# Score products of the first two head pairs from zero-padded parts written in place, second pair rotated on GpSimd

## The chip, the cores and the metric

One core of a Trainium2 chip runs the kernel. The metric is the device time of one execution in microseconds; several executions are timed and their median is taken. One more execution is recorded by the hardware profiler, and all rows of this document come from such a recording. The engines are TensorE (PE, with its weight loads shown apart as PEld), VectorE (DVE), ScalarE (ACT), GpSimd (POOL) and the DMA queue of SyncE (SP). Each engine works through its own instructions in the order in which the program lists them.

## The reference

Attention with rotary embedding on 32 heads (4 batches of 8), 576 positions of 64 channels, followed by a one-of-eight expert layer and a dense layer:

```
q_rot, k_rot = (rotate(q), rotate(k))
scores = scale * np.matmul(q_rot, k_rot.transpose(0, 1, 3, 2))
scores = scores - np.max(scores, axis=-1, keepdims=True)
attn = np.exp(scores)
attn = attn / (np.sum(attn, axis=-1, keepdims=True) + 1e-09)
return np.matmul(attn, v).astype(np.float32)
...
x = _moe_ref(x=x, **moe_kwargs)
return _moe2_ref(x=x, **moe2_kwargs)
```

where `rotate` is `[x1*cos - x2*sin, x1*sin + x2*cos]` on the two halves of the channels. The expert layer sends each of 2304 rows through one expert (512 to 1024 to 512, ReLU); the dense layer is 512 to 2048 to 512 with squared ReLU.

## The kernel before

**Stages.** The program does attention first (about the first 290 us), then the routing and the experts, then the dense layer. The change is in the attention stage alone, in its first microseconds.

**Pairs.** Attention works on 16 pairs of heads, P = 0 to 15. The two heads of a pair stand on partitions 0 to 63 and 64 to 127. The tile `qk` (two buffers) holds keys and queries of a pair, once as they are and once with the halves of the channels swapped, so `rotate` (L189) is three elementwise passes: two products with the table `TB` (L392 in the helper `times`) and a sum (L388 in `plus`). The 128 rotary positions left over from 576 = 512 + 64 of both heads share one block of 128 columns.

**Two parts.** The products on TensorE are taken with numbers of type fp32r, and the precision comes from splitting each rotated value: `high` (L195) writes the rounded value to `XH` on ACT, `low` (L202) writes the remainder to `XL`. A score is H·H + L·H + H·L (query part times key part). A head has only 64 channels, half of the array's rows, so `stack_up` (L212) copies parts by DMA into stacked tiles: `kZ` holds the head's H keys twice, above each other, and `qZ` the H queries above the L queries. One product of `qZ` with `kZ` then gives H·H + L·H, and a second one, of `QH` (H queries of one head, zeros on the other head's partitions) with `XL`, gives H·L. That is 8 DMAs per pair.

**Scores.** `scores(P, s)` (L228) makes one block of 128 queries by 576 keys in two halves of 288 columns, into one of two PSUM buffers `ps`. There are nine blocks per pair: s = 0 to 3 for the first head, 4 to 7 for the second, and 8 for the leftover queries of both (two stacked products and one more a half). Then `smax` (L251, DVE) takes the row maximum and `sexp` (L258, ACT) the exponential, after which the PSUM buffer is free. The exponentials are transposed on TensorE (`turn`, L276), copied to SBUF by DVE or ACT (L292, L294), multiplied with V (`values`, L303), and projected together with the gate weights (`project`, L314).

**Order.** Nothing reorders the program at run time. `prepare` (L140) issues the first pair's work, then every later step is put on a list with a due time (`at`, `OFF`, `pair` = 15.954 a pair) and the list is issued in order of due time. The due time decides only the place in each engine's row. For pair 2 and later, `rotate` runs on POOL, `high` on ACT, `low` on POOL, and `stack_up` on SP. Pairs 0 and 1 are done in `prepare`, with `rotate` on DVE. After the first `high`, 16 products on a scratch tile `warm` (L162) keep TensorE occupied until the first stacked tiles arrive.

Of the kernel before, what the change touches and what calls it, by code (L numbers as in the profile page):

```python
# [10 lines left out]
F32 = mybir.dt.float32  # L11
F32R = mybir.dt.float32r
# [100 lines left out]
def attention(tc, rope, ident, qk, v, w_gate, xd, on_batch, later):  # L113
# [14 lines left out]
    T = {}  # L128
# [11 lines left out]
    def prepare():  # L140
        nc.scalar.dma_start(out=TB[:, :, 0], in_=rope)
        load(0)
        load(1)
        for t in Xs:
            nc.gpsimd.memset(t[:, 576:640], 0.0)
        for t in SS:
            nc.gpsimd.memset(t[:, :, 1:2], 1e-9)
        for two in QH:
            for j in range(2):
                nc.gpsimd.memset(two[j][64 - 64 * j:128 - 64 * j].bitcast(F32), 0.0)  # L150
        nc.gpsimd.memset(R, 0.0)
        for r in range(2):
            d = slice(64 * r, 64 * r + 64)
            nc.gpsimd.tensor_copy(R[d, :, r, 0:64], ident[d, d].unsqueeze(1).broadcast_to([64, 4, 64]))
        for o, lo, hi in ((0, 64, 640), (576, 0, 64)):
            nc.scalar.activation(TB[:, :, 1, o:o + hi - lo], TB[:, :, 0, lo:hi], AF.Copy, scale=0.125)
        for n in range(2):
            rotate(0, n, nc.vector)
            high(0, n)
        w = ppt("warm")  # L160
        for i in range(16):
            nc.tensor.matmul(w, T["hi", 0][:, 0, 0:128], T["hi", 0][:, 0, 0:512], start=True, stop=True)  # L162
        for n in range(2):
            low(0, n, nc.vector)
            stack_up(0, n)
        load(2)
        rotate(1, None, nc.vector)
        high(1)
        low(1)
        load_v(0)  # L170
        for r in range(2):
            nc.sync.dma_start(out=R[64 * r:64 * r + 64, :, r, 64:72], in_=w_gate.rearrange("(g r d) e -> r d g e", r=2, d=64)[r])
        later()
        stack_up(1)

    def load(P):
        t = T["qk", P] = ldp.tile([128, 2, 2, 640], F32, name="qk", tag="qk", bufs=2)
# [7 lines left out]
    def load_v(P):  # L185
        V = T["V", P] = ldp.tile([128, 2, 5, 64], F32, name="V", tag="V", bufs=2)
        nc.sync.dma_start(out=V, in_=v[P].rearrange("p (h c d) -> p h c d", h=2, c=5))

    def rotate(P, n, eng, step=None):  # L189
        x, a = T["qk", P], slice(0, 2) if n is None else slice(n, n + 1)  # L190
        for i, (f, o, y) in enumerate(((times, 0, TB[:, 0, a]), (times, 1, TB[:, 1, a]), (plus, 0, x[:, 1, a]))):
            if step in (None, i):
                f(eng, x[:, o, a], x[:, o, a], y)

    def high(P, n=None):  # L195

        if ("hi", P) not in T:
            T["hi", P] = wp.tile([128, 2, 640], F32R, name="XH", tag="XH", bufs=2)
        a = slice(0, 2) if n is None else slice(n, n + 1)
        nc.scalar.activation(T["hi", P][:, a], T["qk", P][:, 0, a], AF.Copy)  # L200
# [27 lines left out]
    def scores(P, s):  # L228

        t = T["S", P, s] = ps.tile([128, 2, 512], F32, name="ps", tag="ps", bufs=2)  # L230
        if s < 8:
            j, c = divmod(s, 4)
            todo, qs, qh = [j], slice(c * 128, c * 128 + 128), QH[P % 2][j]
            qh = qh[:, qs]
        else:
            todo, qs, qh = [0, 1], slice(512, 640), T["hi", P][:, 1, 512:640]
        k0 = 0 if s in (4, 5, 6, 7) else 64
        for i, j in enumerate(todo):
            Q1, K1 = T["qZ", 2 * P + j], T["kZ", 2 * P + j]
            for u in range(2):  # L240
                nc.tensor.matmul(t[:, u, 0:288], Q1[:, qs], K1[:, k0 + 288 * u:k0 + 288 * u + 288], start=i == 0, stop=False)  # L241
        for u in range(2):
            nc.tensor.matmul(t[:, u, 0:288], qh, T["lo", P][:, 0, k0 + 288 * u:k0 + 288 * u + 288], start=False, stop=True)  # L243
# [103 lines left out]
            at(t, lambda: route(P, t))  # L347

    prepare()
    for P in range(NPAIR):  # L350
        def on(o, f, *args):
            at(OFF["pair"] * P + o, lambda: f(*args))

        if P > 2:
            on(OFF["load"], load, P)
        if P > 0:
            on(OFF["v"], load_v, P)
        if P > 1:
            for i in range(3):
                on(OFF["rope"] + 2.93 * i, rotate, P, None, nc.gpsimd, i)  # L360
            on(OFF["hi"], high, P)
            on(OFF["lo"], low, P)
            on(OFF["z"], stack_up, P)
        for s in range(9):
            on(OFF["S"][s], scores, P, s)
            on(OFF["max"][s], smax, P, s)
            on(OFF["exp"][s], sexp, P, s)
        for un, o, o2 in zip(UNITS, OFF["un"], OFF["out"]):
            on(o, turn, P, un)
            on(o2, turned, P, un)  # L370
        for u in range(2):
            on(OFF["av"][u], values, P, u)
            on(OFF["x"][u], gathered, P, u)
        on(OFF["pj"], project, P)
        on(OFF["fin"], finish, P)
        if P % 4 == 3:
            on(OFF["fin"] + .02, route, P)
# [659 lines left out]
```

## Time and profile before

| | us |
|---|---|
| median of 3 timed executions | 1027.9 (1024.9 to 1030.28) |
| the profiled execution | 1029.81 |
| its span in the trace | 1028.0 |
| PE busy | 981.3 (95%) |
| DVE busy | 547.3 (53%) |
| ACT busy | 420.6 (41%) |
| POOL busy | 310.4 (30%) |

The profiled execution took 1.9 us more than the median, and 1.8 us of it lie outside the span. Busy times are of the whole span; matmul ends are modelled, so a busy PE need not be at its peak. The granted clock (PEclk) is the share of TensorE's full 2.4 GHz: 1.00 is that level, 0.50 is 1.2 GHz. Where the trace has no event of the clock yet, at the start, the column says 1.00 whatever the level was.

### The profile page before, as it was taken

The numbers are of one execution on the slowest core, as the hardware profiler recorded it, in microseconds if no ns is written. First come the engines' busy times: TensorE is split into PE (matmuls) and PEld (weight loads), VectorE is DVE, ScalarE is ACT, GpSimd is POOL, SyncE is SP. The second block draws the span as 40 slices with busy tenths as digits, with TensorE's granted clock in tenths as the row PEclk, the third lists the DMA queues.
The fourth block names the chain that finished last, engine by engine and source line by source line (L and its number), as shares of the span: only waits on it lengthen the run. The fifth ranks groups of instructions, "written<-read, shape, count | busy, mean of one in ns | idle before, by whom it ended". The sixth has DMA issues, their size and how long they took to land. (4 is left out here: it accounts for less than half of the span.)

```text
span 1028.0 us, 15645 instructions
## 1 busy us (share of the span) xinstructions
PE 981.3 (95%) x5624; PEld 838.2 (82%) x5624; DVE 547.3 (53%) x909; ACT 420.6 (41%) x825; POOL 310.4 (30%) x211
## 2 busy tenths in 40 slices
PE   4999999999997999999999988899999999999998
PEld 3788888878785888887878776789999999999997
DVE  5677777777765455554474478852322323323222
ACT  3766675757522233342453344432222222222222
POOL 3786886886112111135342225500000000000000
PEclk8999999999998999999999999999999999999999
DMA  9876877776155633255475422110010010100000
GB/s 280 237 204 183 249 192 210 220 204 169 39 210 153 217 124 124 83 159 201 174 233 178 127 101 84 41 62 1 1 62 1 1 62 1 62 1 1 31 1 32
DMA packets 43408, 121.20 MB, mean 118 GB/s; under 512 B 5936, under 2 KB 5936, under 8 KB 40880
## 3 DMA queue, kind: packets, MB, share of 16 engines
q1 hardware_dynamic: 38544, 104.95, 33.0%
q0 software_dynamic: 4096, 13.63, 4.1%
q10 hardware_dynamic: 672, 1.44, 0.6%
q8 instruction: 47, 0.77, 0.3%
q14 instruction: 49, 0.40, 0.1%
HBM read 79.90 MB, written 14.94 MB: 92 GB/s over the span
## 5 line engine op out<-in xcount | busy, mean ns | idle before, releaser
L894 PE MATMUL o<-Wo,gs 128*128 128x512 f32 x864 | 219.2, 398 | 10.0 <-ACT gs L883 10.0
L876 PE MATMUL h<-xs,Wi 128*128 128x384 f32 x1152 | 219.4, 339 | 2.4 <-DVE Wi L842 1.8
L876 PEld LDWEIGHTS h<-xs,Wi 128*128 128x128 f32 x1152 | 206.6, 189 | 11.3 <-DVE Wi L842 2.1
L894 PEld LDWEIGHTS o<-Wo,gs 128*128 128x128 f32 x864 | 159.5, 189 | 43.6 <-ACT gs L883 12.4
L882 DVE SCALAR_TENSOR_TENSOR g<-h,r 128x384 f32<-128x384 f32 x96 | 53.4, 557 | 196.0 <-ACT r L881 196.0
L258 ACT ACTIVATE e<-ps,mx 128x576 f32<-128x576 f32 x144 | 106.3, 740 | 82.1 <-DVE mx L251 81.9
L251 DVE TENSOR_REDUCE mx<-ps 128x1 f32<-128x576 f32 x144 | 106.0, 753 | 62.4 <-PE ps L243 62.3
L683 PE MATMUL p_h<-W,xs 128*128 128x512 f32 x504 | 124.2, 403 | 5.7 <-ACTq L716 3.3
L881 ACT ACTIVATE r<-h 128x384 f32<-128x384 f32 x96 | 47.0, 490 | 199.4 <-PE h L876 199.4
L705 PE MATMUL p_y<-W,hh 128*128 128x512 f32 x504 | 120.9, 395 | 2.1 <-DVE W L661 0.9
L683 PEld LDWEIGHTS p_h<-W,xs 128*128 128x128 f32 x504 | 95.5, 193 | 26.3 <-ACTq L716 3.5
L705 PEld LDWEIGHTS p_y<-W,hh 128*128 128x128 f32 x504 | 93.1, 188 | 22.0 <-DVE W L661 1.2
L276 PE MATMUL pp<-ident,e 128*128 128x128 f32 x640 | 85.2, 273 | 0.0
L241 PE MATMUL ps<-kZ,qZ 128*128 128x288 f32 x320 | 79.0, 337 | 5.5 <-DMA qZ<-XL 3.0
L884 DVE TENSOR_TENSOR gs<-g,gs 128x384 fp32r<-128x384 f32 x96 | 53.6, 559 | 56.8 <-ACT gs L883 56.8
L883 ACT ACTIVATE gs<-g 128x384 fp32r<-128x384 f32 x96 | 50.5, 526 | 79.9 <-DVE g L882 79.9
L392 POOL TENSOR_TENSOR qk<-qk,TB 128x1280 f32<-128x1280 f32 x28 | 81.4, 2923 | 1.2 <-DMA qk<-in_qk_dram 1.2
L276 PEld LDWEIGHTS pp<-ident,e 128*128 128x128 f32 x640 | 74.9, 141 | 0.5 <-issue 0.4
L303 PE MATMUL av<-eT,V 128*64 128x288 f32 x512 | 69.1, 412 | 0.0
L241 PEld LDWEIGHTS ps<-kZ,qZ 128*128 128x128 f32 x320 | 49.7, 195 | 22.6 <-ACT X L306 6.1
L292 DVE COPY eT<-pp 128x512 f32<-128x512 f32 x96 | 64.4, 685 | 4.1 <-PE pp L276 2.0
L709 POOL DMA_INDIRECT yd<-yo,idx x21 | 21.5, 1025 | 142.7 <-DVE yo L708 135.3
(160 smaller groups left out, 1126.7 us busy)
## 6 DMA issues: line engine op xcount, KB each, us to landing
raw<-in_moe_w_dram SPq DMA_DIRECT2D x44, 512.0 KB, 3.6
qk<-in_qk_dram SPq DMA_DIRECT2D x15, 1280.0 KB, 6.5
kZ<-XH SPq DMA_DIRECT2D x62, 160.0 KB, 2.7
w<-in_moe_w_in_dram SPq DMA_DIRECT2D x8, 1024.0 KB, 7.0
w<-in_moe_w_out_dram SPq DMA_DIRECT2D x8, 1024.0 KB, 8.8
V<-in_v_dram SPq DMA_DIRECT2D x16, 320.0 KB, 3.5
qZ<-XH SPq DMA_DIRECT2D x31, 160.0 KB, 3.5
qZ<-XL SPq DMA_DIRECT2D x31, 160.0 KB, 2.6
```

What stands on the lines that cost most here:

```text
L241: nc.tensor.matmul(t[:, u, 0:288], Q1[:, qs], K1[:, k0 + 288 * u:k0 + 288 * u + 288], start=i == 0, stop=False)
L251: nc.vector.tensor_reduce(small("mx", P, 9)[:, s:s + 1], T["S", P, s][:, :, 0:288], axis=AX.XY, op=ALU.max, negate=True)
L258: nc.scalar.activation(ed.rearrange("p (u n) -> p u n", u=2), T["S", P, s][:, :, 0:288], AF.Exp, bias=T["mx", P][:, s:s + 1], accum_out=SS ...
L276: nc.tensor.transpose(t[:, c * 128:c * 128 + 128], src, ident)
L292: nc.vector.tensor_copy(o, i)
L303: nc.tensor.matmul(t[64 * j:64 * j + 64], V[:, j, kc], eT[:, j, kc, cs] if kc < 4 else eL[:, cs], start=kc == 0, stop=kc == 4)
L392: v.tensor_tensor(out=out, in0=a, in1=b, op=ALU.mult)
L683: nc.tensor.matmul(t[:, 512 * u:512 * u + 512], s[:, a, k], W1[:, b, k, 512 * u:512 * u + 512], start=n == 0, stop=n == 11)
L705: nc.tensor.matmul(t, s[:, a, k], W2[:, b, k], start=n == 0, stop=n == 23)
L876: nc.tensor.matmul(t, W[:, a, k, fs], s[:, c, k], start=n == 0, stop=n == 11)
L884: nc.vector.tensor_sub(gs[:, 1], g, gs[:, 0].bitcast(F32))
L894: nc.tensor.matmul(self.T["o", b][c], gs[:, a, 128 * c:128 * c + 128], W[:, w], start=(f == 0 and n == 0), stop=(f == 15 and n == 2))
```

## The change

For pairs 0 and 1 nothing is stacked any more. `direct_high` casts the first 512 query columns of each head into `QH` on ACT (zeros on the other head's partitions, as before) and the 128 leftover columns into `XH`. `direct_low` writes the remainder of each head's queries into `qZ`, of which the other head's partitions are set to zero by four memsets on POOL, and the leftover columns' remainder into `XL` on POOL. `scores` takes three products a half for these pairs: H·H, L·H and H·L, each with the key parts `XH` or `XL` of both heads, the zeros cancelling the other head. The 16 DMAs of `stack_up` for these pairs go, 4 of them from ACT's queue. The warm products are 12 instead of 16. The second pair is rotated on POOL; its casts and remainders stand in `second_pair`, due at 30.2. The third pair's three rotation passes are due at 30.3 to 30.5 instead of 20.6 to 26.5. The gate weights' and constants' loads are due at 24.0, and V of pair 0 is loaded ahead of `qk` of pair 2.

```diff
-        for n in range(2):
-            rotate(0, n, nc.vector)
-            high(0, n)
+        for P in range(2):
+            for j in range(2):
+                Z = T["qZ", 2 * P + j] = wp.tile([128, 640], F32R, name="qZ", tag="qZ", bufs=4)
+                nc.gpsimd.memset(Z[64 - 64 * j:128 - 64 * j, 0:512].bitcast(F32), 0.0)
+        rotate(0, 0, nc.vector)
+        high(0, 0)
         w = ppt("warm")
-        for i in range(16):
+        for i in range(12):
             nc.tensor.matmul(w, T["hi", 0][:, 0, 0:128], T["hi", 0][:, 0, 0:512], start=True, stop=True)
-        for n in range(2):
-            low(0, n, nc.vector)
-            stack_up(0, n)
-        load(2)
-        rotate(1, None, nc.vector)
-        high(1)
-        low(1)
+        rotate(0, 1, nc.vector)
+        direct_high(0)
+        low(0, 0, nc.vector)
+        direct_low(0, nc.vector)
+        rotate(1, None, nc.gpsimd)
         load_v(0)
+        load(2)
+
+    def second_pair():
+        high(1, 0)
+        direct_high(1)
+        low(1, 0)
+        direct_low(1, nc.gpsimd)
+
+    def direct_high(P):
+        x, h = T["qk", P], T["hi", P]
+        for j in range(2):
+            r = slice(64 * j, 64 * j + 64)
+            nc.scalar.activation(QH[P][j][r], x[r, 0, 1, 0:512], AF.Copy)
+        nc.scalar.activation(h[:, 1, 512:640], x[:, 0, 1, 512:640], AF.Copy)
+
+    def direct_low(P, eng):
+        x = T["qk", P]
+        for j in range(2):
+            r = slice(64 * j, 64 * j + 64)
+            minus(eng, T["qZ", 2 * P + j][r, 0:512], x[r, 0, 1, 0:512], QH[P][j][r].bitcast(F32))
+        minus(nc.gpsimd, T["lo", P][:, 1, 512:640], x[:, 0, 1, 512:640], T["hi", P][:, 1, 512:640].bitcast(F32))
+
+    def gate_weights():
...
-        stack_up(1)
...
         k0 = 0 if s in (4, 5, 6, 7) else 64
+        if P < 2:
+            H, L = T["hi", P], T["lo", P]
+            ql = L[:, 1, 512:640] if s == 8 else T["qZ", 2 * P + j][:, qs]
+            for i, (q1, k1) in enumerate(((qh, H), (ql, H), (qh, L))):
+                for u in range(2):
+                    nc.tensor.matmul(t[:, u, 0:288], q1, k1[:, 0, k0 + 288 * u:k0 + 288 * u + 288], start=i == 0, stop=i == 2)
+            return
...
     prepare()
+    at(24.0, gate_weights)
+    at(30.2, second_pair)
...
-                on(OFF["rope"] + 2.93 * i, rotate, P, None, nc.gpsimd, i)
+                on(OFF["rope"] + 2.93 * i if P > 2 else 30.3 + .1 * i - OFF["pair"] * P, rotate, P, None, nc.gpsimd, i)
```

Three places show what stands in the engines' rows. On ACT between the exponentials of pair 0 (`ss_110`) and those of pair 1 (`ss_111`), before:

```order
L258 ACTIVATE e,ss_110<-ps,mx 128x576 x7
L200 ACTIVATE XH<-qk 128x1280
L258 ACTIVATE e,ss_111<-ps,mx 128x576
L294 ACTIVATE eT<-pp 128x512
L258 ACTIVATE e_325,ss_111<-ps,mx 128x576
```

and in the changed kernel:

```order
L290 ACTIVATE e,ss_110<-ps,mx 128x576 x7
L225 ACTIVATE XH<-qk 128x640
L186 ACTIVATE QH_108<-qk 64x512
L186 ACTIVATE QH_109<-qk 64x512
L187 ACTIVATE XH<-qk 128x128
L225 ACTIVATE XH<-qk 128x1280
L290 ACTIVATE e,ss_111<-ps,mx 128x576
L326 ACTIVATE eT<-pp 128x512
```

The 128x1280 cast is pair 2's `high`, in both; the four casts of pair 1 now stand right ahead of it. On POOL after the memsets, before (the row of L154 is the last of the setup, the first L392 rows are pair 2's rotation):

```order
L154 COPY R<-ident 64x4x64 x2
L208 TENSOR_TENSOR XL<-qk,XH 128x1280
L392 TENSOR_TENSOR qk<-qk,TB 128x1280 x2
L388 TENSOR_TENSOR qk<-qk 128x1280
L208 TENSOR_TENSOR XL<-qk,XH 128x1280
```

and in the changed kernel:

```order
L154 COPY R<-ident 64x4x64 x2
L160 MEMSET qZ 64x512 x4
L418 TENSOR_TENSOR XL<-qk,XH 128x128
L426 TENSOR_TENSOR qk<-qk,TB 128x1280 x2
L422 TENSOR_TENSOR qk<-qk 128x1280
L233 TENSOR_TENSOR XL<-qk,XH 128x640
L418 TENSOR_TENSOR qZ<-qk,QH_108 64x512
L418 TENSOR_TENSOR qZ<-qk,QH_109 64x512
L418 TENSOR_TENSOR XL<-qk,XH 128x128
L426 TENSOR_TENSOR qk<-qk,TB 128x1280 x2
L422 TENSOR_TENSOR qk<-qk 128x1280
L233 TENSOR_TENSOR XL<-qk,XH 128x1280
```

The first rotation is now pair 1's, then come four remainders of pair 1, and pair 2's rotation stands behind them. On PE at the start, before:

```order
L162 MATMUL warm<-XH 128x512 x16
L241 MATMUL ps<-kZ,qZ 128x288 x2
L243 MATMUL ps<-XL,QH_106 128x288 x2
L241 MATMUL ps<-kZ,qZ 128x288 x4
L243 MATMUL ps<-XL,XH 128x288 x2
```

and in the changed kernel:

```order
L165 MATMUL warm<-XH 128x512 x12
L268 MATMUL ps<-XH,QH_106 128x288 x2
L268 MATMUL ps<-XH,qZ 128x288 x2
L268 MATMUL ps<-XL,QH_106 128x288 x2
L268 MATMUL ps<-XH 128x288 x2
L268 MATMUL ps<-XH,XL 128x288 x2
L268 MATMUL ps<-XL,XH 128x288 x2
```

A block of one head has six products instead of four; the block of leftovers keeps six.

## Rows read from the trace of the kernel before

**Rows 1.** Windows: us; busy us (instructions) per engine; clock; DMA share; GB/s.

```profile
66.00:82.00 16.00, 16.00 (x127) 13.03 (x126) 12.02 (x25) 10.46 (x26) 11.61 (x4) 1.00 0.73 202
```

**Rows 2.** Waits of weight loads, 66 to 250 us: total us, times, longest.

```profile
PEld ps L241 <- ACT X L306: 4.8, 11, 0.4
...
PEld ps L241 <- ACT e L258: 1.1, 4, 0.3
...
PEld av L303 <- DVE mx L456: 0.7, 3, 0.2
```

**Rows 3.** Timeline, PE at the opening: start us, us, instructions, [idle before, releaser].

```profile
10.38 6.28 PE L162 MATMUL warm<-XH 128*128 128x512 f32 x16 [10.38 <-ACT XH L200]
...
19.66 0.85 PE L241 MATMUL ps<-kZ,qZ 128*128 128x288 f32 x2 [3.00 <-DMA qZ<-XL]
...
20.30 0.68 PE L243 MATMUL ps<-XL,QH 128*128 128x288 f32 x2
...
20.79 1.55 PE L241 MATMUL ps<-kZ,qZ 128*128 128x288 f32 x4
...
22.70 0.85 PE L241 MATMUL ps<-kZ,qZ 128*128 128x288 f32 x2
...
25.74 0.85 PE L241 MATMUL ps<-kZ,qZ 128*128 128x288 f32 x2
```

**Rows 4.** The warm products: duration in ns, min/median/max, first and last start.

```profile
L162 PE MATMUL warm<-XH x16: 387/632/796, 10.4 to 16.3; 128*128 128x512 f32 x16
```

**Rows 5.** Timeline, VectorE in the first pair's rotation.

```profile
11.07 0.83 DVE L388 TENSOR_TENSOR qk<-qk 128x640 f32<-128x640 f32 x1
```

**Rows 6.** Timeline, ScalarE: a first cast, pair 2's cast, pair 1's first exponential.

```profile
9.59 0.74 ACT L200 ACTIVATE XH<-qk 128x640 fp32r<-128x640 f32 x1 [2.82 <-DVE qk L388]
...
33.79 1.26 ACT L200 ACTIVATE XH<-qk 128x1280 fp32r<-128x1280 f32 x1
34.95 0.73 ACT L258 ACTIVATE e<-ps,mx 128x576 f32<-128x576 f32 x1
```

**Rows 7.** Timeline, PE from pair 0's last blocks to pair 1's third.

```profile
30.61 0.53 PE L241 MATMUL ps<-kZ,qZ 128*128 128x288 f32 x2 [0.90 <-ACT e L258]
...
31.43 0.53 PE L241 MATMUL ps<-kZ,qZ 128*128 128x288 f32 x2
31.80 0.43 PE L243 MATMUL ps<-XL,QH 128*128 128x288 f32 x2
...
33.12 0.53 PE L241 MATMUL ps<-kZ,qZ 128*128 128x288 f32 x2 [0.78 <-ACT e L258]
...
36.22 0.51 PE L241 MATMUL ps<-kZ,qZ 128*128 128x288 f32 x2
```

**Rows 8.** Timeline, GpSimd: pair 2's remainder, then pair 3's rotation.

```profile
35.13 2.93 POOL L208 TENSOR_TENSOR XL<-qk,XH 128x1280 fp32r<-128x1280 f32 x1 [2.94 <-ACT XH L200]
38.02 5.80 POOL L392 TENSOR_TENSOR qk<-qk,TB 128x1280 f32<-128x1280 f32 x2
43.89 2.92 POOL L388 TENSOR_TENSOR qk<-qk 128x1280 f32<-128x1280 f32 x1
```

**Rows 9.** Groups by form, 95 to 215 us, small GpSimd passes: busy us, mean ns.

```profile
L388 POOL TENSOR_TENSOR cum<-cum,oh 128x8 f32<-128x8 f32 x10 | 2.0, 203 | 0.8
...
L392 POOL TENSOR_TENSOR im<-im,consts 128x40 f32<-128x40 f32 x2 | 0.5, 272 | 0.2
```

**Rows 10.** Windows with the granted clock (third number from the end).

```profile
18.50:19.00 0.50, 0.00 (x0) 0.00 (x0) 0.00 (x0) 0.50 (x1) 0.00 (x0) 0.85 0.71 149
...
20.00:28.00 8.00, 7.46 (x28) 6.26 (x28) 3.79 (x5) 3.43 (x9) 6.77 (x3) 0.50 1.02 302
29.09:34.00 4.91, 3.21 (x20) 2.45 (x20) 3.51 (x6) 3.42 (x9) 3.02 (x2) 1.00 1.02 330
...
330.00:334.00 4.00, 4.00 (x13) 3.20 (x12) 0.72 (x2) 0.00 (x0) 0.00 (x0) 0.64 0.89 258
```

**Rows 11.** Timeline, PE in the expert stage, after an idle stretch.

```profile
329.40 6.88 PE L683 MATMUL p_h<-W,xs 128*128 128x512 f32 x22 [1.70 <-DVEq L716]
```

**Rows 12.** The page's part on DMA issues: KB each, us to landing.

```profile
qk<-in_qk_dram SPq DMA_DIRECT2D x15, 1280.0 KB, 6.5
```

More of the change, by code (lines that the diff above doesn't have):

```diff
@@ L156, in prepare @@
             nc.scalar.activation(TB[:, :, 1, o:o + hi - lo], TB[:, :, 0, lo:hi], AF.Copy, scale=0.125)
-        for n in range(2):
-            rotate(0, n, nc.vector)
-            high(0, n)
+        for P in range(2):
[4 more added lines that the diff above has]
+        high(0, 0)
         w = ppt("warm")
-        for i in range(16):
+        for i in range(12):
             nc.tensor.matmul(w, T["hi", 0][:, 0, 0:128], T["hi", 0][:, 0, 0:512], start=True, stop=True)
-        for n in range(2):
-            low(0, n, nc.vector)
-            stack_up(0, n)
-        load(2)
-        rotate(1, None, nc.vector)
-        high(1)
-        low(1)
-        load_v(0)
+        rotate(0, 1, nc.vector)
[3 more added lines that the diff above has]
+        rotate(1, None, nc.gpsimd)
+        load_v(0)
+        load(2)
+    def second_pair():
[16 more added lines that the diff above has]
+    def gate_weights():
         for r in range(2):
```

## Prediction

> **What bounds the kernel now.** I read the busy shares by stretch first, then the waits, then the timelines of the first 50 us. From 34 us to the end of attention TensorE is occupied all the time: a 16 us stretch shows 16.00 us busy for PE against 13.03 for its weight loads, 12.02 for DVE, 10.46 for ACT and 11.61 for POOL [rows 1]. The waits between 66 and 250 us confirm it: the matmuls wait for nobody, and the weight loads wait 4.8, 1.1 and 0.7 us in all for other engines [rows 2]. So a microsecond that TensorE loses or wins before that stream runs is lost or won at the end, as long as the stream is not starved again. The opening is different. TensorE has its first operand at 10.38, runs the warm products to 16.66, then waits 3.00 us at its first score, at 19.66, for the last stacking DMA [rows 3]. The nine blocks of pair 0 then go round a loop: score, maximum, exponential, buffer free, next score; the gaps before 30.61 and 33.12 are waits for the exponential [rows 7]. Two blocks (one on each buffer) take 25.74 - 22.70 = 3.04 us at half clock [rows 3] and 33.12 - 30.61 = 2.51 at full clock [rows 7]; the clock is 0.50 from 20 to 28 and 1.00 from 29.09 [rows 10].
>
> **What the change wins: the start.** The first score no longer waits for stacking. The second rotation of pair 0 ends on DVE at 11.90 [rows 5]. Two casts of 512 columns and one of 128 follow on ACT (a cast of 640 takes 0.74 [rows 6]), and on DVE one remainder of 640 columns and two of 512 at 0.83 for 640 [rows 5]: the operands of the first block stand at 11.90 + 0.83 + 0.66 = 13.4, all of them by 14.1. TensorE is later than that: twelve warm products. The sixteen before started 5.9 us apart from first to last [rows 4], 0.394 each, between 512 columns at 1.2 GHz (0.427) and at 2.4 (0.213), so some 12.6 of the 15 steps ran at the low level and the clock rose near 15.8, whatever the column says there. Twelve at 0.427 end at 10.38 + 5.12 = **15.5**, 4.2 us ahead of before. The 16 stacking DMAs and their issue leave the path with that. TensorE goes straight on with two blocks, so I let the clock rise at about the same time and stay up, as it did from 29.09 to 34 with 3.21 of 4.91 us busy [rows 10].
>
> **The loop of pair 0.** Each block of one head has two products more, 0.13 us each at full clock (an estimate near the low one of its bounds, 288 columns at 2.4 GHz, 0.12, and half of the 0.37 between the first product of a block at 31.43 and its third at 31.80 [rows 7], 0.185), 0.245 at half (20.30 to 20.79 for two) [rows 3]. On the buffer's way round they come once: 2.51 + 0.26 = 2.77 for two blocks. The ninth block starts at 15.5 + 4 x 2.77 = 26.6, plus 0.2 for the first block's cold products: 26.8. Before, the ninth block started at 31.43 and ACT was free for the cast of pair 2 at 33.79 [rows 6, 7], 2.36 later; with the two products 2.62, so ACT comes to `second_pair` at **29.4**. So far the change is 4.4 us ahead.
>
> **What the change puts in the way: pair 1 and pair 2 in one chain.** Between the last exponential of pair 0 and the first of pair 1, ACT's row now holds pair 1's four casts and then pair 2's cast, which it already held before. That cast waits for pair 2's rotation. Before, the rotation was over before ACT came to it: the cast ran at 33.79 behind the exponential, and the exponential of pair 1 at 34.95 [rows 6]. Now the rotation stands on POOL behind pair 1's remainders, and these wait for pair 1's casts, which ACT does only after pair 0's last exponential. POOL's own first rotation is over by 14.1 + 0.46 + 8.8 = 23.4, and then POOL waits six microseconds for ACT. A POOL pass of 1280 columns takes 2.93 and three in a row 46.81 - 38.02 = 8.79 [rows 8]; the smallest, 0.203 for 8 columns and 0.272 for 40 [rows 9], give 0.19 plus 2.14 ns a column, so 640 columns take 1.55, 512 take 1.28, 128 take 0.46. The chain from 29.4:
> cast of 640, 0.74; remainder of 640, 1.55; two of 512, 2.56; 128 columns, 0.46; pair 2's rotation, 8.79; its cast until the exponential may start, 34.95 - 33.79 = 1.16; five handovers at 0.08 (cast end 35.05 to 35.13 [rows 6, 8]), 0.4. Sum 15.7, so pair 1's first exponential starts at **45.1** instead of 34.95. The other three casts lie beside POOL's first remainder and cost nothing.
>
> Queued behind that cast on ACT are all exponentials of pair 1 and ACT's share of the copies. TensorE can do pair 1's first two blocks and the transposes around them, but the third block needs the buffer that this exponential frees. Before it started at 36.22 [rows 7]; now at 45.1 + 0.74 (the exponential's own time) + two handovers = 46.0. **TensorE is 9.8 us behind.** Bounds: with 0.27 for the small pass and no handover time 9.2; with GpSimd's 2.93 spread over the columns without a fixed part 9.4; if pair 0's loop hides the added products, 1.0 less.
>
> **The restart.** TensorE idles some 9 us there. It fell to half level at 18.85 after idling since 16.66 (0.85 in 18.50 to 19.00) [rows 3, 10], so it restarts at half. From a restart to the rise it took 5.4 us at the opening and 3.5 us at 329.40 (0.64 in 330 to 334 puts the rise at 332.9) [rows 4, 10, 11]. Half of that time is lost: 1.75 to 2.7; I take 2.2.
>
> **Added products in the stream.** Pair 1's blocks from the third on lie in the stretch where TensorE sets the pace: seven blocks x 2 x 0.13 = 1.8 us. Bounds 0 (if ACT, nearly full there, hides them) and 1.8.
>
> **What costs nothing.** The SP row: the load of pair 3 waits for pair 1's last remainder, near 34, and V of pair 1, the gate weights and the constants stand behind it. A `qk` load lands in 6.5 us [rows 12], at 41, and is wanted by POOL only after pair 2's remainder, near 49. Pair 2's stacking DMAs wait for the delayed cast anyway, and its first score comes a whole pair later. POOL's memsets (2 us more at 5.4) end before 8, ahead of the first remainder.
>
> **Sum.** 9.8 + 2.2 + 1.8 = 13.8 us more, of which the start's gain of 4.4 is already taken off. Against the profiled execution: 1029.8 + 13.8 = 1043.6. That one lies 1.9 above the median, so for the median 1027.9 + 13.8 = **1041.7**.
>
> A rule of the Trainium skill speaks against moving the rotation: "GPSIMD Engine Reference", section 4.1 Engine selection, calls GpSimd about two times slower than VectorE on two-input elementwise work, and its section 3.1 has 4497 ns for 2048 columns. An estimate from that page is 2.81 us a pass of 1280, and the trace agrees (2.93, rows 8); by the page the chain and the total would be 0.4 us shorter.
>
> **Rivals.**
> *The clock does not hold in the first loop.* Blocks of 1.4 us with under 0.8 us of products might leave TensorE at half level, as from 20 to 28, where it did not rise with 7.46 of 8 us busy [rows 10]. Then the loop is 3.04 + 0.49 = 3.53 for two blocks, 3.0 us more over four rounds, and 0.5 more at the end: +17.3, 1045.2. For it: that stretch. Against it: the level held from 29.09 on with more idling.
> The Trainium skill has this as a rule, in "TensorE: Matmul & The Clock Gate", section "A second HAM failure mode: psum-queue depth-cycling": short idling between groups of matmuls that cycle through PSUM makes the clock swing. No run here shows it yet for this loop.
> *A smaller lag.* ACT hides the added products of pair 1, pair 0's loop hides its own (1.0), the clock is back early (1.75): 8.8 + 1.75 = 10.5, or 1038.4; with a shorter chain down to 1036.
> *Not slower: the stream works the lag off.* If TensorE's full row in pairs 2 to 15 hid slack of about 1 us a pair, 14 pairs would give 13.8 back and the end would stand near 1028. It decides from 13.8/14 = 0.99 us a pair on. Against it: all waits of weight loads for other engines in 184 us are 6.6 us [rows 2], which would leave 7.2 us, and the matmuls' own are none.
> *The change doesn't do what it says*, so that ACT reaches pair 1's exponential without pair 2's rotation: its row excludes that, since engines keep the order of their rows; I give it next to nothing, at the start's 4.4 less the added 1.8: 1025.3.
>
> **How the numbers follow.** Forecast 0.66, clock low in the loop 0.14, smaller lag 0.13, worked off 0.05, not as listed 0.02. A measurement of this kernel can tell about 0.5% from no change, 5.1 us: faster below 1022.8, slower above 1033.0. The first three are slower: 0.93; worked off is same, 0.05; faster 0.02. The range reaches from the smaller lag with a shorter chain, 1036, to the cold loop with the longest restart, 1046.5.
>
> **What would show it.** In the changed kernel's trace: first score near 15.5; clock 1.00 from about 16; pair 1's first cast near 29.4 on ACT; POOL idle from 23 to 30; pair 2's rotation on POOL from about 35 to 44; ACT idle until then with pair 2's cast released by POOL; PE idle about 9 us before pair 1's third block near 46, and half clock for 3 to 5 us behind it; from there the same stream, 14 us late. I am wrong if POOL reaches pair 2's rotation before pair 0's exponentials end, if pair 1's first exponential comes before 40, or if the lag at 46 is not there at 250.

## The result, and the profile after

The changed kernel takes 1043.4 us (median of 4, 1041.16 to 1044.23) against 1028.78 for the kernel before on the same chip: a ratio of 1.0145, 95% interval 1.0111 to 1.0178. The forecast was 1041.7 in a range of 1036 to 1046.5. The profiled execution took 1042.96, its span 1041.2, which is 13.2 us more than the span of before.

The timeline of PE in the changed kernel (start us, us, instructions, idle time before and its releaser), from the warm products to pair 2's first block:

```profile
10.04 4.79 PE L165 MATMUL warm<-XH 128*128 128x512 f32 x12 [10.04 <-ACT XH L225]
14.67 0.43 PE L268 MATMUL ps<-XH,QH 128*128 128x288 f32 x2
...
17.35 0.54 PE L268 MATMUL ps<-XH,QH 128*128 128x288 f32 x2 [0.93 <-ACT e L290]
...
25.71 0.53 PE L268 MATMUL ps<-XH,QH 128*128 128x288 f32 x2 [0.48 <-ACT e L290]
...
31.94 0.85 PE L268 MATMUL ps<-XH,qZ 128*128 128x288 f32 x2 [1.78 <-POOL qZ L418]
...
44.50 0.85 PE L268 MATMUL ps<-XH,QH 128*128 128x288 f32 x2 [6.49 <-ACT e L290]
...
59.98 0.53 PE L273 MATMUL ps<-kZ,qZ 128*128 128x288 f32 x2
```

Read against [rows 3] and [rows 7]: the first score is at 14.67 instead of 19.66, without a wait; pair 1's third block is at 44.50 instead of 36.22, behind the longest wait of the opening. Pair 2's first block is at 59.98 now, and stood at 48.48 before, 11.5 us earlier:

```profile
48.48 0.53 PE L241 MATMUL ps<-kZ,qZ 128*128 128x288 f32 x2
```

From there both kernels run the same stream.

ScalarE between the last exponential of pair 0 and the first of pair 1:

```profile
28.33 0.72 ACT L225 ACTIVATE XH<-qk 128x640 fp32r<-128x640 f32 x1
28.95 1.27 ACT L186 ACTIVATE QH<-qk 64x512 fp32r<-64x512 f32 x2
30.25 0.31 ACT L187 ACTIVATE XH<-qk 128x128 fp32r<-128x128 f32 x1
42.46 1.27 ACT L225 ACTIVATE XH<-qk 128x1280 fp32r<-128x1280 f32 x1 [11.90 <-POOL qk L422]
43.64 0.72 ACT L290 ACTIVATE e<-ps,mx 128x576 f32<-128x576 f32 x1
```

The row to look at is 42.46: pair 2's cast, 11.90 us of waiting for GpSimd, with pair 1's exponential behind it at 43.64 (34.95 before [rows 6]). GpSimd in the same stretch:

```profile
29.13 1.55 POOL L233 TENSOR_TENSOR XL<-qk,XH 128x640 fp32r<-128x640 f32 x1 [6.38 <-ACT XH L225]
30.62 2.61 POOL L418 TENSOR_TENSOR qZ<-qk,QH 64x512 fp32r<-64x512 f32 x2
33.31 0.46 POOL L418 TENSOR_TENSOR XL<-qk,XH 128x128 fp32r<-128x128 f32 x1
33.73 5.74 POOL L426 TENSOR_TENSOR qk<-qk,TB 128x1280 f32<-128x1280 f32 x2
39.55 2.88 POOL L422 TENSOR_TENSOR qk<-qk 128x1280 f32<-128x1280 f32 x1
```

It stands idle 6.38 us for pair 1's first cast, then does the four remainders, and only then pair 2's rotation, to 42.43. The windows (us; busy us and instructions of PE, PEld, DVE, ACT, POOL; clock; DMA share; GB/s):

```profile
14.00:30.00 16.00, 10.28 (x65) 8.60 (x63) 7.42 (x10) 8.95 (x21) 9.54 (x4) 1.00 0.23 82
...
32.00:36.00 4.00, 4.00 (x18) 3.98 (x18) 1.79 (x4) 0.00 (x0) 3.92 (x3) 0.50 0.26 59
...
42.00:48.00 6.00, 3.50 (x15) 3.48 (x16) 0.76 (x1) 4.54 (x10) 4.62 (x3) 0.50 0.49 105
48.00:50.00 2.00, 2.00 (x18) 2.00 (x17) 1.45 (x2) 1.14 (x3) 2.00 (x2) 1.00 0.97 233
66.00:82.00 16.00, 16.00 (x128) 13.06 (x127) 11.89 (x26) 10.53 (x26) 11.16 (x5) 1.00 0.71 196
```

The clock holds through pair 0's loop, falls behind the pauses at pair 1's first products (2.75 us before 29.62, and the 1.78 before 31.94 above), comes back near 38, falls again in the long pause, is at half level when TensorE restarts at 44.50, and is back by 48. In the steady stream PE is as full as before [rows 1].

### The profile page after: what moved, and what is told of

It is laid out like the page before. It is cut to its first block, busy times and chain, and to the rows that moved or that the text cites. A ratio compares the mean times of both kernels' runs of the same rounds, so it can differ in the third digit from the quotient of the medians.

```text
span 1041.2 us, 15685 instructions
## 1 busy us (share of the span) xinstructions
PE 986.1 (95%) x5652; PEld 843.8 (81%) x5652; DVE 543.9 (52%) x907; ACT 422.1 (41%) x830; POOL 322.4 (31%) x222
## 5 line engine op out<-in xcount | busy, mean ns | idle before, releaser
L910 PEld LDWEIGHTS h<-xs,Wi 128*128 128x128 f32 x1152 | 206.2, 189 | 11.3 <-DVE Wi L876 2.2
L308 PE MATMUL pp<-ident,e 128*128 128x128 f32 x640 | 87.3, 278 | 0.0
L426 POOL TENSOR_TENSOR qk<-qk,TB 128x1280 f32<-128x1280 f32 x30 | 87.2, 2924 | 0.0
L273 PE MATMUL ps<-kZ,qZ 128*128 128x288 f32 x280 | 66.8, 328 | 0.2
L730 ACT ACTIVATE hh<-p_t 128x512 fp32r<-128x512 f32 x42 | 22.8, 596 | 79.4 <-PE p_t L729 78.2
```

The source lines that it names most:

```text
L308: nc.tensor.transpose(t[:, c * 128:c * 128 + 128], src, ident)
L426: v.tensor_tensor(out=out, in0=a, in1=b, op=ALU.mult)
L910: nc.tensor.matmul(t, W[:, a, k, fs], s[:, c, k], start=n == 0, stop=n == 11)
```

## The experiments

For each kernel the table has the start of a routing product right behind the attention stage, from its one profile, and its median less the median of before on the same chip. The product is this one, in the changed kernel and before:

```profile
308.44 0.41 PE L510 MATMUL rp<-cum,consts 128*128 128x40 f32 x2 [0.33 <-DVE cum L422]
296.98 0.41 PE L476 MATMUL rp<-cum,consts 128*128 128x40 f32 x2 [0.33 <-DVE cum L388]
```

| | attention ends, us | against 296.98 | median against before, us | ratio, 95% interval |
|---|---|---|---|---|
| changed kernel | 308.44 | +11.5 | +14.6 | 1.0111 to 1.0178 |
| e1_rot2_first | 302.39 | +5.4 | +6.2 | 1.004 to 1.0085 |
| e2_pair1_early | 303.42 | +6.4 | +8.5 | 1.0054 to 1.0117 |
| e3_two_products | 306.13 | +9.2 | +11.3 | 1.0079 to 1.0176 |
| e5_before_late_rot2 | 303.52 | +6.5 | +9.0 | 1.0059 to 1.0137 |
| e4_rot1_on_dve | 311.93 | +15.0 | +18.5 | 1.0159 to 1.021 |
| b0_pair0_only | 295.46 | -1.5 | +1.0 | 0.9996 to 1.0027 |
| b2_pair0_spread | 300.07 | +3.1 | +7.0 | 1.0046 to 1.0083 |
| b3_both_spread | 301.17 | +4.2 | +6.9 | 1.0056 to 1.009 |
| e6_cast_later | 303.96 | +7.0 | +10.8 | 1.0069 to 1.012 |
| b4_early_and_later | 297.76 | +0.8 | +4.2 | 1.0024 to 1.0049 |
| e7_cast2_later | 302.02 | +5.0 | +6.3 | 1.0033 to 1.0071 |
| b5_in_step | 296.69 | -0.3 | +0.4 | 0.9992 to 1.0021 |

The medians lie 0.7 to 3.9 us above what the end of attention says. All of them lie above, which points at the reference that they share, the trace of before: its execution took 1029.81 where the medians of before in these runs are 1026.4 to 1028.8. That is not shown, since no other execution of before has a trace. So the opening is read from the traces, and the size of an effect from the medians; an end of attention slightly below 296.98 is no gain.

The expectations reckon from 1043.4, with before at 1028.78; beside the later runs before measured 1026.4 to 1027.2. So a time is held against its expectation by its difference from the changed kernel: e1_rot2_first -8.4 where -7.5 was expected, e2_pair1_early -6.1 (-5.6), e3_two_products -3.3 (-3.1), e4_rot1_on_dve +3.9 (+2.4). By their bare times the first three lie 0.3 to 0.6 us below their ranges.

**Is it the place of pair 2's rotation?** Theory: it is, by way of pair 2's cast on ScalarE, ahead of pair 1's exponentials. Rivals: the longer chain of pair 1's own operands; the added products; a cost of rotating pair 1 on GpSimd. The first run puts pair 2's rotation ahead of pair 1's remainders:

```diff
-   on(... else 30.3 + .1 * i - OFF["pair"] * P, rotate, P, None, nc.gpsimd, i)
+   on(... else 29.9 + .1 * i - OFF["pair"] * P, rotate, P, None, nc.gpsimd, i)
```

> The changed kernel with one edit: pair 2's rotation is due just ahead of the second pair's work instead of just behind it, so it stands on GpSimd between pair 1's rotation and pair 1's remainders. Theory (ScalarE is held at pair 2's cast by a rotation that stands behind pair 1's remainders): the rotation runs from 22.8 to 31.4 while GpSimd idled before, pair 2's cast follows pair 1's casts at about 31.5, pair 1's remainders come 2.3 us later (first at 31.4 instead of 29.1), its third block near 38.5 instead of 44.5 with the clock already back: 1043.4 - 7.5 = about 1036 (1034 to 1038). Rival (the price is pair 1's own operands, made one after the other, and the added products): pair 1's first block comes 2.3 us later and so does the end, about 1045.7.

It measured 1033.43: 8.4 of the 14.6 us are gone. Its timeline of ScalarE has the cast eleven microseconds earlier:

```profile
31.43 1.27 ACT L225 ACTIVATE XH<-qk 128x1280 fp32r<-128x1280 f32 x1 [1.38 <-POOL qk L422]
36.31 0.74 ACT L290 ACTIVATE e<-ps,mx 128x576 f32<-128x576 f32 x1 [3.62 <-DVE mx L283]
```

TensorE now waits for the other thing in that row of GpSimd, pair 1's remainder:

```profile
34.15 0.85 PE L268 MATMUL ps<-XH,qZ 128*128 128x288 f32 x2 [4.51 <-POOL qZ L418]
```

Both orders put one pair behind the other's work on GpSimd. In this one pair 1's operands wait for 8.7 us of rotation, but the cast waits 1.38 us instead of 11.90, and the third block starts at 39.98 instead of 44.50:

```profile
39.98 0.61 PE L268 MATMUL ps<-XH,QH 128*128 128x288 f32 x2
```

The opposite check puts a late rotation into the kernel before, with nothing else of the change: three dummy passes on GpSimd ahead of pair 2's rotation.

```diff
...
+        for i in range(3):
+            times(nc.gpsimd, DM, TB[:, 0], TB[:, 1])
```

> The kernel before with three more GpSimd passes of 1280 columns (on a tile that nobody reads) ahead of pair 2's rotation; scores, stacking and everything else stay as before. Theory: the rotation ends near 39.8 instead of 32.2, ScalarE waits at pair 2's cast from 33.8 on, pair 1's first exponential starts near 41.0 instead of 34.95, TensorE idles, its clock falls and comes back after 3 to 5 us: 5.7 + 1.8 = 7.5 us more than the kernel before, about 1036.3 (1034 to 1038). Rival (a late cast for pair 2 is hidden, since pair 2's scores start only at 48.5): no change, 1028.8.

1036.24, +9.0 over before where +7.5 was expected. Its rows of ScalarE and PE repeat the pattern of the changed kernel, the cast waiting for GpSimd and the third block for the exponential:

```profile
39.30 1.27 ACT L203 ACTIVATE XH<-qk 128x1280 fp32r<-128x1280 f32 x1 [6.20 <-POOL qk L391]
```

```profile
41.34 0.85 PE L244 MATMUL ps<-kZ,qZ 128*128 128x288 f32 x2 [5.58 <-ACT e L261]
```

So a late rotation alone makes a loss of this kind, without zero-padded parts and without added products. The next run keeps the change and starts pair 1's four casts earlier, between pair 0's exponentials, so that GpSimd does not idle:

```diff
-    at(30.2, second_pair)
+    at(22.7, second_pair)
```

> The changed kernel with one edit: the second pair's casts and remainders are due at 22.7 instead of 30.2, so ScalarE does the four casts after the fifth exponential of pair 0, when pair 1's rotation has just ended. Theory: GpSimd's remainders start at 23.6 instead of 29.1 and everything behind them on the chain moves with it, pair 2's rotation ends near 36.8, pair 1's first exponential starts near 38.0 instead of 43.6; the casts hold pair 0's loop up by 1.9 us, which is hidden behind that chain: 1043.4 - 5.6 = about 1037.8 (1036 to 1039.5). Rival (the order of ScalarE's casts doesn't matter, pair 0's loop sets the pace): 1.9 us slower, about 1045.3.

1035.69, 6.1 us less, as the theory has it. The rotation follows the remainders sooner and the cast waits 7.66 us instead of 11.90; but the four casts in a block delay pair 0's exponentials, and TensorE still waits for pair 1's:

```profile
39.77 0.85 PE L268 MATMUL ps<-XH,QH 128*128 128x288 f32 x2 [6.83 <-ACT e L290]
```

**Is it the added products?** This kernel leaves out the third product, H·L, for pairs 0 and 1:

```diff
-            for i, (q1, k1) in enumerate(((qh, H), (ql, H), (qh, L))):
+            for i, (q1, k1) in enumerate(((qh, H), (ql, H))):
...
```

> The changed kernel without the third product (high queries times low keys) in pairs 0 and 1, so four products a block are left; part of the score is left out. Theory: pair 0's loop shortens by 0.26 us in each of four rounds and at its last block, 1.3 us, and pair 1's seven blocks in the full stream by 0.26 each, 1.8: 1043.4 - 3.1 = about 1040.3 (1039 to 1041.5). ScalarE still waits some 12 us for pair 2's rotation. Rival (the added products are the whole loss): the time falls to that of the kernel before or under it, 1024 to 1029. Rival (they are hidden): no change, 1043.4.

1038.51: with as many products a block as before, and two fewer in the leftover block, +11.3 of the +14.6 are still there, and +9.2 of the +11.5 at the end of attention. The size of the difference is rough, since the intervals overlap (1.0079 to 1.0176 against 1.0111 to 1.0178). The wait is untouched, and a shorter loop of pair 0 only starts it earlier:

```profile
41.27 1.27 ACT L225 ACTIVATE XH<-qk 128x1280 fp32r<-128x1280 f32 x1 [11.90 <-POOL qk L422]
```

**Is it pair 1's rotation on GpSimd?** Back on VectorE:

```diff
-        rotate(1, None, nc.gpsimd)
+        rotate(1, None, nc.vector)
```

> The changed kernel with pair 1's rotation back on VectorE, in the same place of the program (behind pair 0's remainders); nothing else. Theory: that rotation was never on the path (it ended at 22.8, its first reader ran at 28.3). On VectorE it takes 4.4 us, from 13.7 to 18.1, in front of pair 0's first maximum, which ran at 15.7: the loop of pair 0 and the whole chain behind it come 2.4 us later, 1043.4 + 2.4 = about 1045.8, up to 1049 if TensorE's clock falls in the gap. Rival (GpSimd's slow rotation of the second pair is the price): up to 4.4 us faster, about 1039.

1044.91, no better. GpSimd now idles 17.63 us before pair 1's first remainder, so its first rotation was not what made it late; and VectorE's passes delay pair 0's maxima, so the third block comes 2.4 later still:

```profile
31.49 1.54 POOL L233 TENSOR_TENSOR XL<-qk,XH 128x640 fp32r<-128x640 f32 x1 [17.63 <-ACT XH L225]
```

```profile
46.89 0.85 PE L268 MATMUL ps<-XH,QH 128*128 128x288 f32 x2 [7.01 <-ACT e L290]
```

**What is the first half of the change worth?** Only pair 0 gets padded parts; pair 1 stays stacked and pair 2's rotation stays early, both as in the kernel before.

```diff
-        if P < 2:
+        if P < 1:
...
-    at(30.2, second_pair)
```

> One half of the change alone: pair 0's parts written in place with three products, pair 1 as in the kernel before (rotated on VectorE in one piece, remainder on GpSimd, stacked by DMA), pair 2's rotation at its old place. Theory: no cast of pair 2 holds ScalarE up for long, since its rotation ends near 31.2 and ScalarE gets there at about the same time; VectorE's rotation of pair 1 delays pair 0's first maximum to 18.1, the ninth block ends 2.4 us later than in the changed kernel, pair 1's third block starts near 34 instead of 36.2 before: 2 us under the kernel before, about 1025.5 (1023.5 to 1028.5, the upper end if the clock falls while TensorE waits for that maximum). Rival (zero-padded parts lose by themselves): slower than the kernel before by 2 us or more.

1027.43, level with before instead of 2 us below it. (The bare time lies in its range, since before itself measured 1026.41 here.) First scores are early (14.21), but pair 0's first maximum stands behind the rotation on VectorE (18.16), as expected, and ScalarE takes pair 1's cast ahead of the first exponential, which was not:

```profile
18.27 1.27 ACT L222 ACTIVATE XH<-qk 128x1280 fp32r<-128x1280 f32 x1 [5.09 <-DVE qk L418]
```

```profile
20.32 0.85 PE L265 MATMUL ps<-XH,QH 128*128 128x288 f32 x2 [4.35 <-ACT e L287]
...
23.84 0.85 PE L265 MATMUL ps<-XH,QH 128*128 128x288 f32 x2 [0.27 <-ACT e L287]
```

The same mistake of order in small. The cast is the smaller part of it: the first exponential starts at 19.45, and at 18.84 in e4_rot1_on_dve, which has that rotation but not the cast. Then TensorE restarts at half level (0.85 for two products), so that two blocks take 3.52 instead of 2.79. The lead of 5.4 us at the first score is 1.3 at pair 1's third block (34.95 against 36.22). Two kernels were to mend that by spreading pair 1's work between pair 0's steps, one with pair 1 stacked, one with it padded:

```diff
-        rotate(1, None, nc.gpsimd)
+        rotate(1, None, nc.vector, 0)
...
+        at(18.09, lambda: rotate(1, None, nc.vector, 1))
+        at(20.97, lambda: rotate(1, None, nc.vector, 2))
+        at(23.0, lambda: low(1, 0, nc.vector))
...
```

The lines not shown place the other casts and remainders; the gate weights' load and pair 3's load are due later in both.

> As b0_pair0_only, but pair 1's rotation is cut into its three passes, laid on VectorE behind pair 0's remainders, the second and the fourth maximum, and pair 1's remainder is on VectorE too, so GpSimd is free for pair 2's rotation from 21 on. Theory: pair 0's loop is delayed by about 1 us in all instead of 2.4, pair 2's cast waits under 1.5 us, stacking of pair 1 lands near 29 and 32; pair 1's third block starts near 33: 3.2 us under the kernel before, about 1025 (1022.5 to 1027). Rival (the start's gain can't reach the end): equal to the kernel before.

> Both pairs from zero-padded parts as in the change, but pair 1's rotation and remainders cut up on VectorE between the maxima of pair 0, its casts cut up on ScalarE between the exponentials, and pair 2's rotation alone on GpSimd from 21 on. Theory: pair 1's operands stand by 28, pair 2's cast waits under 1.5 us, pair 1's third block starts near 32 to 32.5 instead of 36.2, and the added products of pair 1 give 1.8 us back: 2 us under the kernel before, about 1026 (1023.5 to 1028). Rival (three products a half lose by themselves): slower than the kernel before.

Both missed, at 1033.38 and 1033.35. The reason is in the rows of VectorE and GpSimd. In b3_both_spread, VectorE:

```profile
24.53 2.65 DVE L425 TENSOR_TENSOR XL<-qk,XH 128x640 fp32r<-128x640 f32 x1
...
27.77 2.70 DVE L425 TENSOR_TENSOR qZ<-qk,QH 64x512 fp32r<-64x512 f32 x1
...
31.83 0.69 DVE L425 TENSOR_TENSOR qZ<-qk,QH 64x512 fp32r<-64x512 f32 x1
```

and GpSimd with pair 2's rotation:

```profile
19.44 7.06 POOL L433 TENSOR_TENSOR qk<-qk,TB 128x1280 f32<-128x1280 f32 x2 [5.55 <-DMA qk<-in_qk_dram]
26.58 3.35 POOL L429 TENSOR_TENSOR qk<-qk 128x1280 f32<-128x1280 f32 x1
```

The same 512-column remainder takes 2.70 us while GpSimd rotates and 0.69 after it. A 640-column one takes 2.65 instead of 0.83 [rows 5]. GpSimd's three passes end at 29.93, 10.5 us after they began, instead of 8.79 [rows 8]. VectorE's maxima stand behind those passes, so pair 0's loop stops: TensorE waits 2.98, 2.38 and 1.49 us for exponentials in b3_both_spread, and 2.36 and 4.88 in b2_pair0_spread. The expectations had put VectorE's passes beside GpSimd's at no cost, and that step was wrong.

**Can the order be mended?** Here the casts and remainders of pairs 2 and 3 are due later, behind five exponentials of the pair before, so that ScalarE is free for pair 1:

```diff
-            on(OFF["hi"], high, P)
-            on(OFF["lo"], low, P)
+            late = P in (2, 3)
+            on(OFF["hi"] + 7 * late, high, P)
+            on(OFF["lo"] + 5.6 * late, low, P)
...
```

Only the casts move by 7; the remainders move by 5.6, the stacking by 2.5, and the rotations of pairs 3 and 4 and the loads of pairs 4 and 5 by 3, which the expectation puts as 7 for all.

> The changed kernel, with the casts, remainders, stacking and rotation inputs of pairs 2 and 3 due 7 us later: behind five exponentials of the pair before instead of ahead of them. If the loss comes from ScalarE waiting at pair 2's cast (11.9 us in the changed kernel) with pair 1's exponentials queued behind it: ScalarE goes straight on, pair 1's third block comes near 36.5 instead of 44.5, TensorE has no long idle time, pair 2's first score near 50, and the time is about 1034 us (1032 to 1036.5). If it comes from the longer chain of operands and products itself, or from GpSimd's total, the third block or pair 2's first score stays late and the time stays at 1040 or above.

The near half held: TensorE starts pair 1's third block without a wait and pair 2 8.5 us ahead of the changed kernel, 3.0 behind before:

```profile
37.62 0.57 PE L268 MATMUL ps<-XH,QH 128*128 128x288 f32 x2
...
51.52 0.53 PE L273 MATMUL ps<-kZ,qZ 128*128 128x288 f32 x2
```

The time, 1037.39, lies above its range. From pair 2 to pair 4 the lag on before grows from 3.0 to 7.0 us. GpSimd shows why, with pair 3's remainder waiting for a cast that is now too late, and then pair 4's rotation late behind it:

```profile
61.30 2.92 POOL L233 TENSOR_TENSOR XL<-qk,XH 128x1280 fp32r<-128x1280 f32 x1 [5.09 <-ACT XH L225]
```

```profile
71.60 0.54 PE L273 MATMUL ps<-kZ,qZ 128*128 128x288 f32 x2 [1.23 <-DMA qZ<-XL]
75.04 0.53 PE L273 MATMUL ps<-kZ,qZ 128*128 128x288 f32 x2 [1.77 <-ACT e L290]
```

A second kernel also spreads pair 1's casts on ScalarE between pair 0's exponentials and gives its remainders to GpSimd, where VectorE has no two-input pass to do:

```diff
+        at(22.68, lambda: high(1, 0))
+        at(22.69, lambda: low(1, 0))
...
+            at(t, lambda r=r, j=j: nc.scalar.activation(QH[1][j][r], x[r, 0, 1, 0:512], AF.Copy))
+            at(t + .01, lambda r=r, j=j: minus(nc.gpsimd, T["qZ", 2 + j][r, 0:512], x[r, 0, 1, 0:512], ...))
...
```

> As e6_cast_later, and pair 1's casts are spread on ScalarE behind four of pair 0's exponentials, with its remainders on GpSimd right behind its own rotation, so that VectorE does no two-input pass while GpSimd rotates. Theory: first block of pair 1 near 28, third block near 31 (36.22 before), seven added products 1.8 us, so 2 to 3.7 us below the kernel before: about 1024.5 us (1022.5 to 1027). Rival: GpSimd, which then has two rotations and pair 1's remainders ahead of pair 2's, brings pair 2's operands late, and the time is equal to the kernel before or above it (1028 to 1034).

1030.79, above the range. Here too the opening did as expected: pair 1's first block comes at 27.11 and pair 2's at 44.30, 4.2 us ahead of before, and then pairs 2 and 3 lose it: TensorE waits 1.28, 1.32 and 1.66 us, and ScalarE 4.02 at pair 4's cast.

```profile
44.30 0.53 PE L278 MATMUL ps<-kZ,qZ 128*128 128x288 f32 x2
```

The last two kernels are these two with pair 3's cast, remainder and stacking less late, and pair 4's cast and remainder a little later than before:

```diff
-            late = P in (2, 3)
-            on(OFF["hi"] + 7 * late, high, P)
+            on(OFF["hi"] + {2: 7, 3: 4.5, 4: 1.4}.get(P, 0), high, P)
...
```

> As e6_cast_later, but only pair 2's cast stays five exponentials late; pair 3's goes behind three of pair 2's exponentials, pair 4's behind one of pair 3's. In e6_cast_later GpSimd sat idle 5.09 us before pair 3's remainder, waiting for the cast that had been put too late, the next cast then waited 4.04 us for GpSimd's rotation, and TensorE 1.23 and 1.77 us. If that gave the rest of its loss: those waits go, and the time is 3 to 4 us below e6_cast_later, near 1033.5 us (1032 to 1035). Rival: GpSimd's total work is the limit in pairs 2 to 4, the waits only move, and the time stays within 1 us of e6_cast_later (1037.4).

> As b4_early_and_later, with the same two due times mended (pair 3's cast behind three of pair 2's exponentials, pair 4's behind one of pair 3's). There TensorE waited 1.32 and 1.66 us in pair 3, ScalarE 4.02 us. Theory: without them about 4 us below b4_early_and_later's 1030.8, that is 1026.5 us (1024.5 to 1028.5), level with the kernel before: seven added products (1.8 us) are paid out of the earlier start. Rival: GpSimd's total is the limit, the waits only move, 1030 or above.

1032.93 and 1027.0: 4.5 and 3.8 us less, both as the theory has it and not as the rival, GpSimd's total. In e7_cast2_later GpSimd's wait ahead of pair 3's remainder is 2.72 instead of 5.09:

```profile
59.30 2.92 POOL L233 TENSOR_TENSOR XL<-qk,XH 128x1280 fp32r<-128x1280 f32 x1 [2.72 <-ACT XH L225]
```

b5_in_step is level with before (interval 0.9992 to 1.0021), not faster. Its rows tell where its lead of 3.7 us at pair 2 (44.82 against 48.48) goes: pair 2's stacking comes 1.33 late, and pair 5's rotation waits 3.58 us on GpSimd for a load whose due time I had moved back. At the blocks of leftovers the lead is 2.1 us in pair 2, 1.4 in pair 4, and 0.3 from pair 5 on.

```profile
44.82 0.53 PE L278 MATMUL ps<-kZ,qZ 128*128 128x288 f32 x2
...
48.09 0.50 PE L278 MATMUL ps<-kZ,qZ 128*128 128x288 f32 x2 [1.33 <-DMA qZ<-XL]
```

```profile
73.31 5.80 POOL L431 TENSOR_TENSOR qk<-qk,TB 128x1280 f32<-128x1280 f32 x2 [3.58 <-DMA qk<-in_qk_dram]
```

That a load issued on time would bring a gain was not tried. No kernel of this study beats the kernel before.

## Why the prediction was right, step by step

**The mechanism.** Right in every link of the chain: pair 2's cast waits on ScalarE for GpSimd (11.90 us), pair 1's exponential behind it, TensorE's third block behind that, and the lag of 11.5 us at pair 2 is still 11.5 at the end of attention (308.44 against 296.98). The runs back it from three sides: taking the rotation forward gives back 8.4 us, the late rotation alone costs the kernel before 9.0, and with the cast moved behind the exponentials the third block comes without a wait (37.62). Not forecast were the two pauses at pair 1's first blocks (2.75 and 1.78 us), so that these ran at half level and TensorE idled 6.49 us before the third block instead of some 9.

**The start.** Forecast 15.5, measured 14.67. The term that was off is "twelve at 0.427": the program began 0.34 earlier (10.04 against 10.38), and the twelve took 14.67 - 10.04 = 4.63 us, not 5.12, since the clock was up before the first score, whose two products take 0.27 from the start. Half a microsecond is within chance here: the same twelve products took from 4.18 us (b0_pair0_only, 10.03 to 14.21) to 5.29 (b2_pair0_spread, 10.26 to 15.55). The count of transfers that go is wrong in the text ahead: `stack_up` issues ten DMAs a pair (two `kZ`, two `qZ` and one `QH` a head), so 20 go and 5 of them from ACT's queue, not 16 and 4. No term of the sum rests on it.

**The loop.** 2.77 for two blocks forecast, (25.71 - 17.35) / 3 = 2.79 measured, with the clock at 1.00. The rival of a cold loop did not come about: 10.28 of 16 us busy with pauses of up to 0.93 us, and the level held. In b0_pair0_only the loop did run cold at first (0.50 from 20 to 26), but it entered so, out of a pause of 4.35 us. The rule of the Trainium skill that I had named beside that rival ("TensorE: Matmul & The Clock Gate", section "A second HAM failure mode: psum-queue depth-cycling") did not show in this loop.

**The chain.** ScalarE came to pair 1's casts at 28.33, not 29.4; that is the earlier start again, plus a first block without cold products. From there to the exponential 15.31 us, forecast 15.7. The lag at the third block was 44.50 - 36.22 = 8.3 instead of 9.8.

**Restart and added products.** From the third block to pair 2 the changed kernel takes 59.98 - 44.50 = 15.48 and before 48.48 - 36.22 = 12.26. Of the 3.22, seven blocks with two products of 0.13 would be 1.8, as forecast; the rest, 1.4, is the restart, which I had at 2.2. Two runs show the parts by themselves. e6_cast_later has the added products, and its clock is up from 37.8: 51.52 - 37.62 = 13.90, so they cost 1.6. e5_before_late_rot2 has the restart without them: 55.23 - 41.34 = 13.89, 1.6 as well.

**The sum.** These are 8.3 + 1.8 + 1.4 = 11.5 instead of 13.8. That the profiled execution came out at 1042.96 against 1043.6 is in part luck. It owes 1.7 us to something not forecast: the lag, 11.3 when the dense layer begins (608.48 against 597.16), is 12.9 at its last products (1030.54 against 1017.65). One place where it grows, in the dense layer of the changed kernel:

```profile
682.18 3.34 PE L910 MATMUL h<-xs,Wi 128*128 128x384 f32 x11 [1.80 <-DVE Wi L876]
```

and the same eleven products in the kernel before:

```profile
670.90 2.21 PE L876 MATMUL h<-xs,Wi 128*128 128x384 f32 x11 [1.75 <-DVE Wi L842]
```

Both had waited about as long; the one group ran mostly at the low level (mean clock 0.61 from 682 to 686), the other at the high one. Nothing points at the change here. From the routing product of the table to the end of the span the fourteen traces take 728.0 to 732.8 us, with the same program: 731.0 before, 732.8 in the changed kernel, but 728.3, 729.7 and 728.0 in e3_two_products, e4_rot1_on_dve and e5_before_late_rot2, which are late too. Why the level falls in one execution and not in another stays open. The ends of the stated range do not follow from its terms either: 1045.2 and the longer restart (2.7 for 2.2) give 1045.7, not 1046.5, and no sum leads to 1036; the median of 1043.4 lies inside both ways.

**The rival on the other side.** The stream worked nothing off: the lag is 11.5 us at the block of leftovers of pair 2 (62.03 against 50.53) and at that of pair 15 (278.62 against 267.16). The weight loads of the changed kernel, too, wait 4.8 and 1.1 us for ScalarE between 66 and 250, as in [rows 2].

## What to carry to other kernels

In a row that is worked in order, a step for the next tile must not stand ahead of the current tile's steps unless its input is sure to be there; when a change makes that input later, move the step that waits for it as well, and then look at the next tile for the same thing. A gain at the start is worth only what is left of it when the stream that fills the slowest engine begins: here five microseconds at the first score were a loss at pair 2, and after the order was mended the added products and late transfers still ate them. Before work goes to an engine with free time, see what the other engines do at that moment: here passes of VectorE and GpSimd stretched each other.

## What the runs showed of the hardware that I had not expected

- VectorE passes with two inputs in SBUF stretch when GpSimd rotates: 0.69 to 2.70 us (512 columns), 0.83 to 2.65 (640). Each ends shortly after the GpSimd pass that was running: GpSimd ends one at 26.50 and VectorE's 24.53 pass ends at 27.18; GpSimd ends the next at 29.93 and VectorE's 27.77 pass ends at 30.47, each some 0.6 later, about its own length. That fits waiting for a whole pass of the other engine. GpSimd's three passes took 1.7 us longer in all. Row maxima, which read PSUM, kept their 0.74 to 0.76 beside it. The Trainium skill states this in "SBUF — State Buffer", section "Who interferes with whom": a VectorE instruction with two SBUF inputs contends with a GpSimd instruction that reads SBUF, and the shared port is an exclusive lock. The trace agrees; I had left it out of two expectations.
- TensorE kept its full level through pauses of 0.93 us in pair 0's loop, was at half level behind pauses of 2.75 and 1.78 us (0.50 from 32 to 36), and again behind the one of 6.49; there it came back some 3.5 us after the restart. A single pause of 2.76 us in e4_rot1_on_dve left the level up (two products in 0.53 behind it). I had counted the long pause only, though the shorter ones were in the chain that I described.
